# A gated mix of attention and a ReGLU block on one core: padded DRAM rows, down's weights and rows fetched in another order, the last normalisation on GpSimd

## The chip, the cores and the metric

The kernel runs on one core of one Trainium2 chip. The metric is the time of one execution on the device in microseconds; the time before is the median of three runs, 1238.48 us (1235.03 to 1239.87). One more execution was taken with the hardware profiler; all numbers of the trace come from that one.

The core has a matrix engine (TensorE, PE in the profile), VectorE (DVE), ScalarE (ACT) and GpSimd (POOL), each with its own queue of instructions worked off in order, and SyncE (SP), which here only issues DMA transfers, also in order. [...]

## What is computed

```python
# S = 2048 tokens, D = 448, H = 16 heads of 28, F = 1792; all float32
g = sigmoid((x * gate_w).sum(-1, keepdims=True))
q, k, v = heads(A_x @ A_wqkv)
a = concat_heads(softmax(q @ k.T * 28 ** -0.5) @ v) @ A_wo
gate, up = x @ B_W_gate, x @ B_W_up
b = ((gate * (gate > 0)) * up) @ B_W_down
out = g * a + (1 - g) * b
```

## The kernel before

Matrix products of float32 accuracy are made from two parts of each operand. The high part is a rounded copy (`act_high`, line 120, on ScalarE), the low part the rest (`low`, line 126, on VectorE, or `pool_low`, line 129, on GpSimd). Each operand thus passes two engines before TensorE can use it: "split" in what follows.

Three stages follow each other:

1. **Projections** (0 to some 140 us). `qk` (line 420) and `vproj` make q, k and v from X. q and k are split and written to a DRAM tile `qk_d` (line 133), one row of 2048 tokens (8 KB) for each high and each low part of a dimension. The blocks 1 to 3 of X, already split, are written to DRAM tiles `x_d` (line 135) of 128 rows of 8 KB, in 4 chunks of 512 tokens.
2. **Attention with the gate and up products mixed in** (to some 1035 us). There are 32 "visits", two for each head; the string in `ROUNDS` gives the order of small steps of one visit: scores, maxima, exponentials, the product with V, and one pass (`x`) of the gate or up product. At the first score step of an even visit `loads` issues `load_k` (line 164) and `load_q` (line 169) for a later head: K's 56 rows are read twice into partitions 0 to 55 and 56 to 111, Q's rows four times 28. The split gate and up weights `wg` are reloaded from DRAM (`load_f`, line 583) once their buffer is free. At the end of a block of tokens `gu_mm` (line 591) reads the next block of X back, chunk by chunk. The hidden rows h are written to `h_d`.
3. **Down and output** (line 810 on). `down(i)` multiplies hidden row block i (56 of them: 4 blocks of 512 tokens by 14 blocks of 128 features) with down's weights of its feature block: 4 groups of 3 matmuls. `wout(tb, t)` multiplies normalised head outputs with the output weights, 11 matmuls each; `result` mixes both with the gate and writes out.

What orders stage 3 is the list `todo` (line 914), worked off once while the program is built: each engine's queue holds its share of the list in the list's order. Its steps are:

- `fetch_d(i)` (line 868): SyncE loads the raw weight block `wdr` i, if i is below 14, and the hidden row block `hr` i. Each of the two has 4 buffers, so number i waits until number i - 4 has been split.
- `split_wd(i)` (line 700): high part of weight block i on ScalarE, low part on GpSimd. Blocks 0 to 3 were loaded and split before the stage.
- `split_d(i)` (line 876): high part of row block i on ScalarE, low part on VectorE, into one of 3 buffers `hh`, so that it waits for `down(i - 3)`.
- `load_wo` (line 814) and `split_wo` (line 821): output weights, three transfers into `wor`, then split on ScalarE and GpSimd.
- `row_sums(15)` (line 659), `spread(15)` (line 665), `normalise(15)` (line 671): for the last head, the reciprocal of the softmax sums on VectorE, written to DRAM and read back to all partitions (`rb`, four transfers), and the product with them. For the heads before, `normalise` runs on GpSimd; for the last one on VectorE. It ends with four transfers to `o_d`.
- `fetch_o(tb)` (line 829), `split_o(tb, c)` (line 836): the normalised outputs of all heads for 512 tokens, three transfers into `or` (one buffer), split in two halves on ScalarE and GpSimd into `on`.

`before(i, ...)` (line 928) inserts steps ahead of `down(i)`. As the list stands, `normalise(15)` lies ahead of `down(3)`, `fetch_o(0)` ahead of `down(4)`, its splits ahead of `down(6)` and `down(7)`, and the products `wout(0, 0..3)` ahead of `down(9)` to `down(12)`.

Of the kernel before, what the change touches and what calls it, by code (L numbers as in the profile page):

```python
# [8 lines left out]
F32 = mybir.dt.float32  # L9
# [3 lines left out]
OP = mybir.AluOpType  # L13
# [5 lines left out]
P = 128  # L19
S = 2048  # L20
D = 448
H = 16
# [4 lines left out]
NF = F // P  # L27
NB = 4
TB = 512
# [55 lines left out]
def gated_mix_kernel(ctx, tc, x, wq, wo, wgu, wd, out):  # L85
    nc = tc.nc
# [4 lines left out]
    dram = ctx.enter_context(tc.tile_pool(name="dram", bufs=1, space=DRAM))  # L91
# [28 lines left out]
    def act_high(dst, src):  # L120
        nc.scalar.activation(dst, src, AF.Copy)  # L121
# [7 lines left out]
    def pool_low(dst, src, high):  # L129
        nc.gpsimd.tensor_tensor(dst, src, f32(high), op=OP.subtract)  # L130


    qk_d = dram.tile([2 * D, 2, S], F32, name="qk_d")

    x_d = {(tb, r): dram.tile([P, 4, TB], F32, name=f"x_d_{tb}_{r}") for tb in range(1, NB) for r in range(2)}

    v_d = {g: dram.tile([P, NK, 4, 32], F32, name=f"v_d_{g}") for g in (2, 3)}

# [3 lines left out]
    h_d = {}  # L142
# [421 lines left out]
    done = starts[-1] // (2 * NT)  # L564
# [52 lines left out]
    OS, LS = {}, {}  # L617
# [52 lines left out]

    def normalise(h):
        o = OS.pop(h)
        (nc.gpsimd if h < H - 1 else nc.vector).tensor_tensor(o, o, LS.pop(h), op=OP.mult)
        for j in range(NB):
            nc.sync.dma_start(o_d[DH * h:DH * (h + 1), j * TB:(j + 1) * TB], o[32 * j:32 * j + DH])

# [5 lines left out]
    DR, HK, early = {}, {}, []  # L682
# [52 lines left out]
    for v, order in enumerate(ROUNDS):  # L735
# [4 lines left out]
        for o in order:  # L740
# [12 lines left out]
            elif o == "x":  # L753
                i, half, n = passes.pop(0)
# [3 lines left out]
                if n == NT - 1:  # L758
                    i, half, ps = units.pop()
# [15 lines left out]
            elif o == "b":  # L775
                block_min()
            elif o == "A":
                all_max()
            elif o == "g":
                take_max()  # L780
            elif o == "N":
                if v > 1 and v % 2:
                    normalise(v // 2 - 1)
            elif o == "e":
                take_exp()
            elif o in "cf":
                rescale(v, "cf".index(o))
            elif o == "D":
                split_wd(len(early))
                early.append(o)  # L790
            elif o == "l":
                sends.pop()()
            elif o == "u":
                split_f(0, act_high, pool_low, (1,))
                QS.append(last_q("Q2"))
                for a, b in ((GD, 12), (GD + 12, 4)):
                    nc.sync.dma_start(f32(QS[2])[a:a + b].rearrange("p j t -> p (j t)"), Q[1][GD + 2:GD + 2 + b].bitcast(F32))
                load_k(2)
                load_q(2)
                fetch_f(2)  # L800
                parts = 2
            elif o in "PQ":
                pv(v, "PQ".index(o))
# [7 lines left out]
    pf = ctx.enter_context(tc.tile_pool(name="ffn", bufs=1))  # L811
    WO = pf.tile([P, 7, D], F32R, name="WO")

    def load_wo():
        r = pf.tile([P, 4, TB], F32, name="wor", tag="on0", bufs=2)
        nc.sync.dma_start(r[:, 0:3, :D], wo_d[0:3 * P].rearrange("(c p) n -> p c n", p=P))
        for a in (0, 64):
            nc.sync.dma_start(r[a:a + 64, 3, :D], wo_d[3 * P:])
        return r[:, :, :D]

    def split_wo(r):
        act_high(WO[:, 0:3], r[:, 0:3])
        pool_low(WO[:, 3:6], r[:, 0:3], WO[:, 0:3])
        act_high(WO[:, 6], r[:, 3])
        pool_low(WO[64:, 6], r[64:, 3], WO[64:, 6])
# [39 lines left out]

    WD.append(pf.tile([P, NF - 4, 2, D], F32R, name="WD"))

    def fetch_d(i):

        if i < NF:  # L870
            DR[i] = pf.tile([P, D], F32, name=f"wdr_{i}", tag="wdr", bufs=4)
            nc.sync.dma_start(DR[i], wd[i * P:(i + 1) * P])
        HK[i] = pf.tile([P, TB], F32, name=f"hr_{i}", tag="hr", bufs=4)
        nc.sync.dma_start(HK[i], h_d[i])

    def split_d(i):
        HH[i] = pf.tile([P, 2, TB], F32R, name=f"hh_{i}", tag="hh", bufs=3)
# [20 lines left out]
    def down(i):  # L898
# [6 lines left out]
        if f == NF - 1:  # L905
# [5 lines left out]


    wor = []
    todo = [(fetch_d, 4), (fetch_d, 5), (split_d, 0), (row_sums, H - 1), (split_d, 1), (fetch_d, 6), (fetch_d, 7),
            (lambda: wor.append(load_wo()),), (gate_up, done), (split_wd, 4), (spread, H - 1),
            (split_wd, 5), (gate_up, done + 1)]
    for i in range(NB * NF):
        if i >= 4 and i + 4 < NB * NF:
            todo.append((fetch_d, i + 4))
        if i + 2 < NB * NF:  # L920
            if 4 < i + 2 < NF - 1:
                todo.append((split_wd, i + 3))
            todo.append((split_d, i + 2))
        todo.append((down, i))
        if done + 2 + i < NB * NF:
            todo.append((gate_up, done + 2 + i))

    def before(i, *new):
        n = todo.index((down, i))
        todo[n:n] = new  # L930


    before(3, (normalise, H - 1))
    for tb, load, split, at in ((0, 4, (6, 7), (9, 10, 11, 12)), (1, 9, (13, 14), (16, 17, 18, 19)), (2, 21, (23, 25), (28,) * 4),
                                (3, 35, (37, 39), (42,) * 4)):
        before(load, (fetch_o, tb))
        for k, i in enumerate(split):
            before(i, (split_o, tb, 2 * k))
        for t, i in enumerate(at):
            before(i, (wout, tb, t))  # L940
    before(1, (lambda: split_wo(wor[0]),))
    for f, *a in todo:
        f(*a)

# [36 lines left out]
```

## Time and profile before

| | |
|---|---|
| median of three runs | 1238.48 us (1235.03 to 1239.87) |
| the profiled execution: its time | 1232.55 us |
| its span, first to last instruction | 1230.8 us |
| granted TensorE clock, mean | 0.996 |
| TensorE busy | 1198.2 us (97%) |
| VectorE, ScalarE, GpSimd busy | 908.3, 871.0, 750.9 us |
| moved by DMA | 178.36 MB, mean 145 GB/s |

How to read it: a group or timeline row names the line of the kernel, the engine, the operation, then out<-in by the program's tile names. In brackets or behind the last bar stands how long the engine was idle just before, and whose work ended that. `SPq` is SyncE issuing a transfer: its duration is the issue alone, not the transfer. A row "A <- B: 7.8, 1, 7.8" of the waits says that A waited for B 7.8 us in total, once, 7.8 us at the longest. In a table of windows each row gives the busy time of PE, weight loads, VectorE, ScalarE and GpSimd in that stretch, then the granted clock, the share of time that the 16 DMA engines were busy, and the GB/s that they moved.

### The profile page before, as it was taken

The numbers are of one execution on the slowest core, as the hardware profiler recorded it, in microseconds if no ns is written. First come the engines' busy times: TensorE is split into PE (matmuls) and PEld (weight loads), VectorE is DVE, ScalarE is ACT, GpSimd is POOL, SyncE is SP. The second block draws the span as 40 slices with busy tenths as digits, with TensorE's granted clock in tenths as the row PEclk, the third lists the DMA queues.
The fourth block names the chain that finished last, engine by engine and source line by source line (L and its number), as shares of the span: only waits on it lengthen the run. The fifth ranks groups of instructions, "written<-read, shape, count | busy, mean of one in ns | idle before, by whom it ended". The sixth has DMA issues, their size and how long they took to land.

```text
span 1230.8 us, 16835 instructions
## 1 busy us (share of the span) xinstructions
PE 1198.2 (97%) x6183; PEld 825.4 (67%) x6183; DVE 908.3 (74%) x1178; ACT 871.0 (71%) x956; POOL 750.9 (61%) x327
## 2 busy tenths in 40 slices
PE   9999989999999999999999999999999999899998
PEld 6888655565666666656665666566666566789998
DVE  6466788989898888878887988798888553543342
ACT  5322779898999788877887888888887896422121
POOL 4221477989898676666675766767666776441020
PEclk9999999999999999999999999999999999899999
DMA  9846454354445435252545434344423235543432
GB/s 319 301 171 257 148 187 133 123 155 147 160 116 171 131 122 157 71 147 85 147 133 167 122 114 116 116 138 160 137 97 102 96 105 177 185 141 112 138 111 81
DMA packets 63486, 178.36 MB, mean 145 GB/s; under 512 B 13050, under 2 KB 19650, under 8 KB 58754
## 3 DMA queue, kind: packets, MB, share of 16 engines
q1 hardware_dynamic: 56812, 151.53, 40.3%
q0 software_dynamic: 6160, 25.30, 5.4%
q8 instruction: 49, 0.80, 0.3%
q10 hardware_dynamic: 432, 0.46, 0.1%
q14 instruction: 33, 0.27, 0.1%
HBM read 118.58 MB, written 58.87 MB: 144 GB/s over the span
## 4 chain that ended last, share of the span: by engine, by line
PE 81%; DMA 7%; DVE 4%; ACT 3%; issue 1%; SPq 1%; POOL 1%; DVEq 0%; ACTq 0%; POOLq 0%
PE gu L594 18%; PE po L647 18%; PE s L302 16%; PE acc L885 9%; PE sm L200 9%; PE qk L423 5%; DMA wg<-ws_d 4%; PE wo L848 3%; PE v L441 3%; DVE r L256 2%; DVE mx L204 1%; ACT P L308 1%; ACT P L306 1%; DMA X<-x_d 1%; DMA wgr<-wgu 1%
## 5 line engine op out<-in xcount | busy, mean ns | idle before, releaser
L285 POOL TENSOR_TENSOR P<-P,rm 128x2048 f32<-128x2048 f32 x102 | 469.9, 4627 | 110.1 <-DVE rm L279 84.8
L594 PE MATMUL gu<-X,wg 128*128 128x512 f32 x1232 | 365.0, 395 | 6.4 <-DMA wg<-ws_d 6.3
L204 DVE TENSOR_REDUCE mx<-sm 128x1 f32<-128x1024 f32 x256 | 303.1, 1216 | 48.1 <-PE sm L200 46.6
L302 PE MATMUL s<-Q,K 128*128 128x512 f32 x1024 | 319.9, 407 | 7.7 <-ACT P L306 4.0
L594 PEld LDWEIGHTS gu<-X,wg 128*128 128x128 f32 x1232 | 231.7, 188 | 64.3 <-DMA wg<-ws_d 8.5
L302 PEld LDWEIGHTS s<-Q,K 128*128 128x128 f32 x1024 | 181.6, 188 | 99.5 <-ACT P L306 17.0
L308 ACT ACTIVATE P<-s 128x1024 f32<-128x1024 f32 x204 | 200.6, 1031 | 62.4 <-PE s L302 60.6
L647 PE MATMUL po<-P,V 128*32 128x512 f32 x1640 | 227.1, 594 | 0.4 <-ACT rl L604 0.4
L306 ACT ACTIVATE P<-s 128x1024 f32<-128x1024 f32 x206 | 198.8, 1033 | 11.2 <-PE s L302 9.8
L292 ACT ACTIVATE P<-P 128x2048 f32<-128x2048 f32 x102 | 195.8, 1923 | 2.7 <-POOL P L285 2.4
L200 PE MATMUL sm<-K,Q 128*128 128x512 f32 x520 | 167.5, 406 | 7.9 <-DVE rm L279 2.2
L256 DVE SCALAR_TENSOR_TENSOR r<-s,r 128x1024 f32<-128x1024 f32 x124 | 151.8, 1225 | 23.2 <-ACT P L308 10.6
L647 PEld LDWEIGHTS po<-P,V 128*32 128x32 f32 x1640 | 63.1, 110 | 116.6 <-issue 111.9
L647 PE MATMUL po<-V 128*32 128x512 f32 x408 | 135.6, 594 | 0.0
L285 POOL TENSOR_TENSOR V<-V,rm 128x2048 f32<-128x2048 f32 x24 | 111.0, 4633 | 25.3 <-DVE rm L279 19.0
L200 PEld LDWEIGHTS sm<-K,Q 128*128 128x128 f32 x520 | 91.0, 188 | 49.0 <-ACT P L306 14.8
L127 DVE TENSOR_TENSOR hh<-hr,hh 128x512 fp32r<-128x512 f32 x52 | 51.5, 994 | 86.7 <-ACT hh L121 78.2
L121 ACT ACTIVATE hh<-hr 128x512 fp32r<-128x512 f32 x52 | 32.8, 631 | 112.4 <-PE acc L885 112.4
L885 PE MATMUL acc<-WD,hh 128*128 128x448 f32 x480 | 102.9, 374 | 4.3 <-ACT hh L121 3.1
L885 PEld LDWEIGHTS acc<-WD,hh 128*128 128x128 f32 x480 | 92.4, 193 | 13.2 <-ACT hh L121 3.9
L256 DVE SCALAR_TENSOR_TENSOR r<-s,P 128x1024 f32<-128x1024 f32 x50 | 61.1, 1221 | 39.3 <-ACT P L308 38.8
L271 DVE TRANSPOSE_TENSOR_REDUCE mn<-r 128x32 f32<-128x1024 f32 x63 | 78.2, 1241 | 1.4
(88 smaller groups left out, 1139.1 us busy)
## 6 DMA issues: line engine op xcount, KB each, us to landing
wg<-ws_d SPq DMA_DIRECT2D x42, 896.0 KB
K<-qk_d SPq DMA_DIRECT2D x32, 448.0 KB
Q<-qk_d SPq DMA_DIRECT2D x64, 224.0 KB
h_d<-h SPq DMA_DIRECT2D x56, 256.0 KB
hr<-h_d SPq DMA_DIRECT2D x52, 256.0 KB
ws_d<-wg SPq DMA_DIRECT2D x14, 896.0 KB
qk_d<-st POOLq DMA_DIRECT2D x21, 512.0 KB, 3.1
wgr<-wgu SPq DMA_DIRECT2D x13, 512.0 KB
```

The source lines that it names most:

```text
L200: nc.tensor.matmul(ps[:, c, :], Q[h][:, u * P:(u + 1) * P], K[h % 3][:, k0:k0 + TB], start=True, stop=True)
L204: nc.vector.tensor_reduce(to, ps, axis=AX.XY, op=OP.max)
L256: nc.vector.scalar_tensor_tensor(r, ps, -1.0, before, op0=OP.mult, op1=OP.min)
L271: nc.vector.tensor_reduce(MN[:, 1:3], R2.pop((v, j)).rearrange("p a (b r) -> p a b r", r=32), axis=AX.X, op=OP.min, apply_transpose=True)
L285: nc.gpsimd.tensor_tensor(QUAD[q], QUAD[q], m, op=OP.subtract)
L292: nc.scalar.activation(q, q, AF.Exp, scale=-SCALE)
L302: nc.tensor.matmul(ps[:, c], K[h % 3][:, k * P:(k + 1) * P], Q[h][:, j * TB:(j + 1) * TB], start=True, stop=True)
L306: nc.scalar.activation(dst, ps, AF.Exp, scale=SCALE)
L308: nc.scalar.activation(dst, ps, AF.Copy, scale=-1.0)
L594: nc.tensor.matmul(ps, WS[i][:, s, a], xf(i // NF, b), start=(n == 0), stop=(n == NT - 1))
L647: nc.tensor.matmul(po[32 * j:32 * j + 32], V[:, h // 4 % 2, k, h % 4], AT.pop((v, k, j)), start=(k == k0), stop=(k == k0 + NK // 2 - 1))
L885: nc.tensor.matmul(ACC[i // NF][t][:, :D], HH[i][:, a, t * P:(t + 1) * P], wd_high_low(f, b), start=(f == 0 and n == 0), stop=(f == NF - 1 ...
```

## The change

- The rows of `qk_d` and `x_d` in DRAM become 512 bytes (128 floats) longer; the added bytes are neither written nor read.
- `normalise(15)` runs on GpSimd, and stands ahead of `split_wo` and `down(1)` instead of ahead of `down(3)`.
- `fetch_d` is parted into `fetch_w` (raw weights) and `fetch_h` (hidden rows), each placed directly behind the split that frees its buffer. Weight blocks 8 and 9 are fetched right behind `split_wd(4)` and `split_wd(5)`, later ones three `down`s earlier in the list than before; rows 6 and 7 come behind `load_wo` and behind weight block 9, later ones two `down`s earlier in the list.
- `fetch_o(0)` and its two splits, and `fetch_o(1)`, stand one `down` earlier in the list; the places of `wout` among the `down`s are the same.

```diff
-    qk_d = dram.tile([2 * D, 2, S], F32, name="qk_d")
-    x_d = {(tb, r): dram.tile([P, 4, TB], F32, name=f"x_d_{tb}_{r}") for tb in range(1, NB) for r in range(2)}
+    qk_d = dram.tile([2 * D, 2, S + P], F32, name="qk_d")[:, :, :S]
+    x_d = {(tb, r): dram.tile([P, 4 * TB + P], F32, name=f"x_d_{tb}_{r}")[:, :4 * TB].rearrange("p (c t) -> p c t", c=4) for tb in range(1, NB) for r in range(2)}
...
-        (nc.gpsimd if h < H - 1 else nc.vector).tensor_tensor(o, o, LS.pop(h), op=OP.mult)
+        nc.gpsimd.tensor_tensor(o, o, LS.pop(h), op=OP.mult)
...
-    def fetch_d(i):
+    def fetch_w(i):
         if i < NF:
             DR[i] = pf.tile([P, D], F32, name=f"wdr_{i}", tag="wdr", bufs=4)
             nc.sync.dma_start(DR[i], wd[i * P:(i + 1) * P])
-        HK[i] = pf.tile([P, TB], F32, name=f"hr_{i}", tag="hr", bufs=4)
-        nc.sync.dma_start(HK[i], h_d[i])
+
+    def fetch_h(i):
+        if i < NB * NF:
+            HK[i] = pf.tile([P, TB], F32, name=f"hr_{i}", tag="hr", bufs=4)
+            nc.sync.dma_start(HK[i], h_d[i])
...
-    todo = [(fetch_d, 4), (fetch_d, 5), (split_d, 0), (row_sums, H - 1), (split_d, 1), (fetch_d, 6), (fetch_d, 7),
-            (lambda: wor.append(load_wo()),), (gate_up, done), (split_wd, 4), (spread, H - 1),
-            (split_wd, 5), (gate_up, done + 1)]
+    todo = [(fetch_w, 4), (fetch_h, 4), (fetch_w, 5), (fetch_h, 5), (split_d, 0), (row_sums, H - 1), (split_d, 1),
+            (fetch_w, 6), (fetch_w, 7), (lambda: wor.append(load_wo()),), (fetch_h, 6), (gate_up, done), (spread, H - 1),
+            (split_wd, 4), (fetch_w, 8), (split_wd, 5), (fetch_w, 9), (fetch_h, 7), (gate_up, done + 1)]
     for i in range(NB * NF):
-        if i >= 4 and i + 4 < NB * NF:
-            todo.append((fetch_d, i + 4))
+        if 5 < i + 3 < NF:
+            todo += [(split_wd, i + 3), (fetch_w, i + 7)]
         if i + 2 < NB * NF:
-            if 4 < i + 2 < NF - 1:
-                todo.append((split_wd, i + 3))
             todo.append((split_d, i + 2))
+        if i >= 2:
+            todo.append((fetch_h, i + 6))
         todo.append((down, i))
...
-    before(3, (normalise, H - 1))
-    for tb, load, split, at in ((0, 4, (6, 7), (9, 10, 11, 12)), (1, 9, (13, 14), (16, 17, 18, 19)), (2, 21, (23, 25), (28,) * 4),
+    for tb, load, split, at in ((0, 3, (5, 6), (9, 10, 11, 12)), (1, 8, (13, 14), (16, 17, 18, 19)), (2, 21, (23, 25), (28,) * 4),
                                 (3, 35, (37, 39), (42,) * 4)):
...
-    before(1, (lambda: split_wo(wor[0]),))
+    before(1, (normalise, H - 1), (lambda: split_wo(wor[0]),))
```

## The prediction

> **What bounds the kernel now.** I read the page's busy times and clock line first, then the matmul timeline of the last stage, then who was late there (ScalarE, then SyncE's queue), and last the stage with q and k.
>
> ```profile
> span 1230.8 us, 16835 instructions
> ...
> PE 1198.2 (97%) x6183; PEld 825.4 (67%) x6183; DVE 908.3 (74%) x1178; ACT 871.0 (71%) x956; POOL 750.9 (61%) x327
> ...
> PEclk9999999999999999999999999999999999899999
> ```
>
> TensorE is busy for 1198.2 of 1230.8 us, so only some 32 us of idle time can be won, plus what a lowered clock costs (the 8 near the end of the clock line). The change touches two places where TensorE stands. The first is the start of the down stage. In the timeline the columns are start, duration, then the instruction, and in brackets the idle time before it:
>
> ```profile
> 1055.20 7.46 PE L885 MATMUL acc<-WD,hh 128*128 128x448 f32 x36
> 1063.88 0.68 PE L885 MATMUL acc<-WD,hh 128*128 128x448 f32 x2 [1.22 <-ACT hh L121]
> 1065.12 3.84 PE L885 MATMUL acc<-WD,hh 128*128 128x448 f32 x10 [0.57 <-DVE hh L127]
> 1070.86 0.68 PE L885 MATMUL acc<-WD,hh 128*128 128x448 f32 x2 [1.89 <-ACT hh L121]
> 1072.11 3.77 PE L885 MATMUL acc<-WD,hh 128*128 128x448 f32 x10 [0.58 <-DVE hh L127]
> 1075.72 2.02 PE L848 MATMUL wo<-WO,on 128*128 128x448 f32 x9
> 1078.70 0.68 PE L848 MATMUL wo<-WO,on 128*128 128x448 f32 x2 [0.95 <-POOL on L130]
> 1079.21 0.97 PE L885 MATMUL acc<-WD,hh 128*128 128x448 f32 x4
> ...
> 1066.00:1070.00 4.00, 2.97 (x9) 2.31 (x7) 0.00 (x0) 0.28 (x1) 0.00 (x0) 0.68 0.97 293
> ```
>
> Each `down` is 12 matmuls. The 36 of `down` 4 to 6 take 7.46 us, 2.43 us for 12 with the overlap off. `down(7)`, `down(8)` and the first output product then fill 1062.66 to 1079.21: 16.55 us for 2.43 + 2.43 + 2.23 (11 matmuls) = 7.1 us of work. So 9.45 us are lost, 5.21 of them idle. The rest is mostly the clock: the last row (a window; behind the five engines stand clock, DMA share and GB/s) has a granted clock of 0.68, and ten matmuls take 3.84 instead of about 2.1 us, 1.7 too many. ScalarE tells what is late:
>
> ```profile
> 1062.73 0.58 ACT L121 ACTIVATE WD<-wdr 128x448 fp32r<-128x448 f32 x1 [6.70 <-DMA wdr<-wd]
> 1063.21 0.61 ACT L121 ACTIVATE hh<-hr 128x512 fp32r<-128x512 f32 x1
> 1069.71 0.58 ACT L121 ACTIVATE WD<-wdr 128x448 fp32r<-128x448 f32 x1 [5.89 <-DMA wdr<-wd]
> 1070.72 1.04 ACT L121 ACTIVATE on<-or 128x1024 fp32r<-128x1024 f32 x1
> ```
>
> ScalarE waits twice for a raw block of down's weights (blocks 8 and 9), and the split of the row that TensorE needs is queued behind. SyncE says why they are late:
>
> ```profile
> 1042.03 0.43 SPq L816 DMA_DIRECT2D wor<-wo_d  x1
> 1044.72 2.74 SPq L669 DMA_DIRECT2D rb<-l_d  x4
> 1049.88 0.34 SPq L613 DMA_DIRECT2D h_d<-h  x1
> 1058.05 1.98 SPq L675 DMA_DIRECT2D o_d<-os  x4
> 1060.13 0.36 SPq L872 DMA_DIRECT2D wdr<-wd  x1
> 1061.01 0.42 SPq L832 DMA_DIRECT2D or<-o_d  x1
> 1062.71 0.54 SPq L872 DMA_DIRECT2D wdr<-wd  x1
> 1068.01 0.32 SPq L874 DMA_DIRECT2D hr<-h_d  x1
> ...
> SPq L675 <- DVE os L673: 7.8, 1, 7.8
> SPq L874 <- DMA or<-o_d: 2.5, 2, 2.2
> SPq L613 <- DMA wor<-wo_d: 2.4, 1, 2.4
> ```
>
> SyncE stands 7.8 us for the last normalisation, with the load of block 8 queued behind it (issued 1060.13, used 1062.73: 2.6 us), and block 9 follows the 1 MB of `or` (three transfers, 768 KB and twice 128 KB by their tiles; block 9 issued 1062.71, used 1069.71: 7.0 us). The last row shows a second limit: `h_d` at 1049.88 is the eighth transfer after the first of `wor` (1042.03) and waited until that had landed, so this queue has eight in flight at most.
>
> **The change, part by part.** *Weights further ahead.* `fetch_w(8)` and `(9)` now stand in the queue directly behind `spread`, before the normalised rows. Their buffers are those of blocks 4 and 5, split long before. They are eighth after the second and third part of `wor`. Without two row loads (512 KB) ahead of it `wor` lands somewhat earlier than 1049.8, so blocks 8 and 9 issue at about 1049 and land 2.6 us later, by 1052; both waits on `wdr` (6.70 and 5.89 us of ScalarE) go. The row loads wait for a `hh` split of the same round, but the row is used four rounds (9.7 us) later, so that wait is covered by four `down`s.
>
> *The normalisation on GpSimd.*
>
> ```profile
> 1056.38 1.65 DVE L673 TENSOR_TENSOR os<-os,rb 128x512 f32<-128x512 f32 x1
> ...
> 1029.46 1.29 POOL L673 TENSOR_TENSOR os<-os,rb 128x512 f32<-128x512 f32 x1
> ...
> 1051.24 4.67 POOL L130 TENSOR_TENSOR WO<-wor,WO 128x1344 fp32r<-128x1344 f32 x2 [7.26 <-ACT WO L121]
> 1055.99 3.05 POOL L130 TENSOR_TENSOR WD<-wdr,WD 128x448 fp32r<-128x448 f32 x2
> ...
> 1071.84 2.47 POOL L130 TENSOR_TENSOR on<-or,on 128x1024 fp32r<-128x1024 f32 x1 [0.32 <-ACT on L121]
> ```
>
> It costs 1.29 us there and waits only for `rb`. No row shows that landing: it lies between the end of the issue plus 2.6 us (1050.1) and 1056.38, when VectorE used it. I take 1050.4, since VectorE was busy with other rows until then. Behind it on GpSimd wait the low halves of `WO` (4.67) and of weight blocks 6 and 7 (3.05 for two): 1050.4 + 1.29 + 4.67 + 1.5 = 1057.9 for block 6. TensorE needs it at `down(6)`, 1060.2, so 2.3 us of cover hide the move. The four writes to `o_d` issue at 1051.7 to 1053.7 instead of 1058.05.
>
> *The head outputs' load.* `fetch_o(0)` stands behind `fetch_w(10)`, which needs block 6's buffer (1057.9), and `fetch_h(9)`: `or` issues at about 1058.8, 2.2 us earlier than now. Its landing: 7.0 us (1061.01 to 1068.01, where SyncE waited for it) is the upper end; the lower is 4.2 us, an estimate of 2.1 (the 2.6 of block 8 without the 0.5 that its 224 KB take at the 440 GB/s quoted below) and 768 KB at 440 GB/s. I take 5.7: the four `o_d` writes are no longer just ahead of it. So it lands at 1064.5.
>
> *What is late next.* `split_o(0, 0)` moved one `down` forward, so on ScalarE weight block 9 and row 8 are now queued behind its wait for `or`. ScalarE: `on` until 1065.5, `WD`, then `hh` done at 1066.6, its low half on VectorE 1.2 later (the idle brackets above: about 0.6 between pairs), 1067.8. TensorE ends `down(7)` at 1065.1, stands 1.5 us, does two matmuls, stands again, and ends `down(8)` at 1067.8 + 2.05 = 1069.85. Twice such a stop was followed by the low clock (1.7 us); I charge half, 0.85: 1070.7. GpSimd meanwhile: first half of `on` 1065.5 + 2.47, block 9 1.4, second half 2.6: 1072.0; the tenth matmul of the product comes at 1070.7 + 1.8 = 1072.5, covered. The product ends at 1070.7 + 2.23 = 1072.95 instead of 1079.21: **6.2 us won**. With `or` after 4.2 us, everything is 1.5 earlier, without the low clock and with a 0.4 wait for GpSimd: 8.1. With 7.0 us and the full clock cost: 4.1.
>
> *The longer rows.* The second place:
>
> ```profile
> 413.40 0.87 SPq L167 DMA_DIRECT2D K<-qk_d  x2
> 415.03 3.16 SPq L175 DMA_DIRECT2D Q<-qk_d  x4
> 418.29 0.48 SPq L586 DMA_DIRECT2D wg<-ws_d  x1
> ...
> 418.50:423.00 4.50, 4.50 (x20) 3.20 (x18) 4.29 (x9) 4.50 (x7) 1.64 (x1) 1.00 0.99 226
> 434.50:436.50 2.00, 2.00 (x26) 0.55 (x20) 1.66 (x2) 2.00 (x3) 0.00 (x0) 1.00 1.05 440
> 1035.00:1036.00 1.00, 1.00 (x6) 0.81 (x5) 0.30 (x1) 0.74 (x2) 0.67 (x1) 1.00 0.87 165
> ...
> PE gu L594 <- DMA wg<-ws_d: 6.3, 5, 2.1
> PE sm L200 <- DMA X<-x_d: 1.3, 2, 0.6
> ```
>
> While a head's K and Q come in (1.79 MB, about 9 us), the 16 DMA engines are fully busy and move 226 GB/s; `wg` is queued behind, and five times TensorE waits for it. The bounds of the padding are nothing and 6.3 + 1.3 = 7.6 us. The nearest row for a row pitch that is a power of two is the second window: the reload of V, 8 KB rows at a pitch of 8 KB, runs at 440 GB/s. It differs from K and Q in filling 128 partitions where they fill 56 or 28, not in its pitch. So I take 0.
>
> [...]
>
> **The sum.** Against the profiled execution's 1232.55 us: minus 6.2 gives 1226.35. That execution lies 5.93 below the median shown (1238.48, of 1235.03 to 1239.87), so I put the median at 1232.3.
>
> **The rivals.** *The padding works too.* For it: the third window above, the start of a `wg` load into 128 partitions with 7 KB rows, moves only 165 GB/s, so not the partitions alone make a load slow, and engines that start together might meet in DRAM. Against it: the V row. It would take away the 7.6: 1224.7.
>
> *The stall only moves.* GpSimd's chain holds `fetch_w(10)`, and with it `or`, and ScalarE is stuck on `or` with row 8 behind it. If `rb` lands 2 us late and `or` takes 7.0, the gain is 2.1: 1236.4. Against it: nothing in the queue at that time but two small loads.
>
> *Slower: the gaps between rows cost bandwidth.* K's 56 rows are one run of DRAM now and are apart afterwards. Should K and Q fall to the 165 GB/s of the third window, their 9 us become 12.3, and each of the five waits grows by 3.3: 16.5 us lost, 1248.8. It decides from about 2.5 us a wait (12.4 in all, the 6.2 won and 6.2 more). Against it: every row is still 8 KB in one piece.
>
> **How the numbers follow.** About 0.5% (6.2 us) is what a measurement can tell from no change, and the forecast lies on that line. Chances: forecast 55% (its own range 1230.4 to 1234.4), padding too 28%, stall moves 9%, slower 8%. Faster: half the forecast and nearly all of the second, 0.54; same: the other half and the third, 0.36; slower 0.10 with what I overlook. The range 1223.5 to 1240 leaves out the slower case and the best end of the second.
>
> **What would show it.** Right: no wait of ScalarE on `wdr`, blocks 8 and 9 issued before `o_d`, the normalisation on GpSimd near 1051, `or` issued near 1059, one stop of TensorE of about 2 us before `down(8)` with row 8 behind `on`, and the first output product done near 1073. The five `wg` waits unchanged at about 6 us and some 226 GB/s in the K and Q windows mean that the padding does nothing; under 2 us of such waits mean that the first rival holds. The forecast is wrong if TensorE stands elsewhere in the down stage, or if those waits grow.

## The result and the profile after

| | before | after |
|---|---|---|
| median (lowest to highest), 12 runs each | 1236.65 us (1230.54 to 1239.87) | 1236.12 us (1232.35 to 1239.58) |
| ratio of after to before, 95% interval | | 1.0002 (0.9983 to 1.0021) |
| the profiled execution: time, span | 1232.55, 1230.8 us | 1237.06, 1235.2 us |

The change moves nothing that can be measured. The time lies inside the predicted range, 3.8 us above the forecast, and close to what the rival "the stall only moves" gave (1236.4); how much of that is luck is said with the prediction's steps further down. The profiled execution of before was a quick one among its own runs, that of after was not, so in what follows times of the last stage are counted from the first matmul of `down(0)`, which is 1045.47 us in before and 1047.74 us in after.

The page of after, its busy times and clock line:

```profile
span 1235.2 us, 16834 instructions
...
PE 1200.2 (97%) x6183; PEld 825.6 (67%) x6183; DVE 910.1 (74%) x1177; ACT 870.6 (70%) x956; POOL 752.9 (61%) x328
...
PEclk9999999999999999999999999999999999899999
```

The dip near the end of the clock line is still there. TensorE's timeline in the down stage shows why (start, duration, instruction, and in brackets the idle time before it):

```profile
1072.61 1.11 PE L889 MATMUL acc<-WD,hh 128*128 128x448 f32 x2 [5.25 <-ACT hh L121]
1074.61 4.10 PE L889 MATMUL acc<-WD,hh 128*128 128x448 f32 x10 [0.89 <-DVE hh L127]
1078.51 2.51 PE L848 MATMUL wo<-WO,on 128*128 128x448 f32 x11
```

Before, TensorE stood at five places of this stretch, 5.21 us together; now it stands at two, 6.14 us together, both at `down(8)`: ahead of its first matmul and behind its second. The first output product ended 33.9 us after the start of `down(0)` (1079.38); now it ends at 1081.02, after 33.3 us. ScalarE's timeline, then its waits in the stretch from 1047 to 1085 us (total, times, longest), say what is late:

```profile
1060.10 0.63 ACT L121 ACTIVATE hh<-hr 128x512 fp32r<-128x512 f32 x1 [1.33 <-PE acc L889]
1070.51 1.06 ACT L121 ACTIVATE on<-or 128x1024 fp32r<-128x1024 f32 x1 [9.78 <-DMA or<-o_d]
1071.47 0.56 ACT L121 ACTIVATE WD<-wdr 128x448 fp32r<-128x448 f32 x1
1071.94 0.61 ACT L121 ACTIVATE hh<-hr 128x512 fp32r<-128x512 f32 x1
```
```profile
ACT on L121 <- DMA or<-o_d: 9.8, 1, 9.8
```

The two waits for raw weights, 6.70 and 5.89 us, are gone, as intended. In their place is one of 9.78 us for `or`, and the split of row 8, which TensorE needs for `down(8)`, stands third behind it. SyncE's timeline and its waits show how `or` came to be late:

```profile
1043.63 0.43 SPq L816 DMA_DIRECT2D wor<-wo_d  x1
1044.11 1.15 SPq L818 DMA_DIRECT2D wor<-wo_d  x2
1045.31 0.58 SPq L878 DMA_DIRECT2D hr<-h_d  x1
1045.99 1.04 SPq L613 DMA_DIRECT2D h_d<-h  x1
1047.13 4.17 SPq L669 DMA_DIRECT2D rb<-l_d  x4
1051.40 0.84 SPq L872 DMA_DIRECT2D wdr<-wd  x2
...
1055.62 1.61 SPq L675 DMA_DIRECT2D o_d<-os  x4
1057.32 0.34 SPq L878 DMA_DIRECT2D hr<-h_d  x1
1061.79 0.36 SPq L872 DMA_DIRECT2D wdr<-wd  x1
1062.24 0.38 SPq L878 DMA_DIRECT2D hr<-h_d  x1
1062.67 0.42 SPq L832 DMA_DIRECT2D or<-o_d  x1
```
```profile
SPq L872 <- POOL WD L130: 12.4, 2, 8.4
...
SPq L669 <- DMA wor<-wo_d: 2.3, 1, 2.3
```

Count the transfers from the first of `wor` (1043.63): three of `wor`, row 6, the store of h, and three parts of `rb` are eight. The fourth part of `rb` is the ninth, and waited 2.3 us for the first of `wor` to land (1050.98). In before row 6 did not stand there, the four parts were the fifth to the eighth, and the transfer that waited (2.4 us) was the ninth, a store of h. The wait in after did not make `rb` late, though. The trace also records when each transfer landed. The first three parts, which had not waited, landed 5.5 to 6.0 us after the start of `down(0)`, the fourth 6.3 us after it (1054.05). In before the four landed after 5.8 to 6.4 us (the last at 1051.85), so no earlier. GpSimd, which needs all four, starts its product 0.25 us behind the last of them, and then does one thing after another:

```profile
1054.30 1.29 POOL L673 TENSOR_TENSOR os<-os,rb 128x512 f32<-128x512 f32 x1 [8.04 <-DVE hh L127]
1055.55 4.66 POOL L130 TENSOR_TENSOR WO<-wor,WO 128x1344 fp32r<-128x1344 f32 x2
1060.29 4.14 POOL L130 TENSOR_TENSOR WD<-wdr,WD 128x448 fp32r<-128x448 f32 x3
```

The bracket of the first row names a split on VectorE, which ended at 1054.16, 0.1 us behind the landing of `rb`. ScalarE had the high part of `WO` ready at 1052.79, so GpSimd stood 1.5 us with that work at hand, because the product was ahead of it in its queue.

Weight block 10 (issued 1061.79) takes the buffer of block 6, whose low half is the first of those three `WD`. So SyncE stood from 1057.66 (the end of the row load at 1057.32) to 1061.79 (the shorter of the two waits for `POOL WD`, 12.4 - 8.4 = 4.0 us), with `or` queued behind, though the stores to `o_d` had been issued by 1057.23. The windows, with five engines, clock, DMA share and GB/s:

```profile
1058.00:1062.00 4.00, 4.00 (x22) 3.70 (x21) 3.99 (x3) 1.40 (x3) 3.84 (x4) 1.00 0.26 71
1062.70:1070.50 7.80, 4.66 (x23) 3.97 (x22) 0.00 (x0) 0.00 (x0) 1.73 (x2) 1.00 0.88 253
1071.00:1078.50 7.50, 5.00 (x12) 3.97 (x13) 5.91 (x3) 4.94 (x9) 6.86 (x4) 0.56 0.37 125
1080.00:1110.00 30.00, 30.00 (x146) 27.24 (x146) 13.19 (x16) 6.33 (x10) 10.63 (x9) 1.00 0.46 145
418.50:423.00 4.50, 4.50 (x20) 3.19 (x18) 4.29 (x9) 4.50 (x7) 1.64 (x1) 1.00 0.97 217
```

First row: while SyncE waited, the DMA engines were idle three quarters of the time. Second: then they were 0.88 busy, with block 10 and row 9 (224 and 256 KB, by their tiles) just ahead of `or`. Third: after the stop the clock was 0.56. The fourth is used in the last section. The last row is that of the K and Q load, about as before (226 GB/s); V's reload still moves 433 GB/s. So are the waits for gate and up weights (7.2 us in all, against 6.3):

```profile
PE gu L594 <- DMA wg<-ws_d: 7.2, 5, 2.1
```

### The profile page after: what moved, and what is told of

Its sections match the earlier page's. It is cut to its first block, busy times and chain, and to the rows that moved or that the text cites. A ratio compares the mean times of both kernels' runs of the same rounds, so it can differ in the third digit from the quotient of the medians.

```text
span 1235.2 us, 16834 instructions
## 1 busy us (share of the span) xinstructions
PE 1200.2 (97%) x6183; PEld 825.6 (67%) x6183; DVE 910.1 (74%) x1177; ACT 870.6 (70%) x956; POOL 752.9 (61%) x328
## 4 chain that ended last, share of the span: by engine, by line
PE 81%; DMA 6%; DVE 6%; ACT 4%; issue 1%; POOL 1%; SPq 1%; DVEq 0%; ACTq 0%; POOLq 0%
PE gu L594 18%; PE po L647 18%; PE s L302 16%; PE sm L200 9%; PE acc L889 8%; PE qk L423 5%; DMA wg<-ws_d 4%; PE wo L848 3%; PE v L441 3%; DVE r L256 2%; DVE mx L204 1%; ACT P L308 1%; ACT P L306 1%; DMA wor<-wo_d 1%; DMA or<-o_d 1%
## 5 line engine op out<-in xcount | busy, mean ns | idle before, releaser
L256 DVE SCALAR_TENSOR_TENSOR r<-s,r 128x1024 f32<-128x1024 f32 x124 | 151.8, 1225 | 23.2 <-ACT P L308 10.6
L200 PEld LDWEIGHTS sm<-K,Q 128*128 128x128 f32 x520 | 91.1, 189 | 49.6 <-ACT P L306 15.5
L127 DVE TENSOR_TENSOR hh<-hr,hh 128x512 fp32r<-128x512 f32 x52 | 54.4, 1056 | 86.9 <-ACT hh L121 86.9
```

The source lines that it names most:

```text
L200: nc.tensor.matmul(ps[:, c, :], Q[h][:, u * P:(u + 1) * P], K[h % 3][:, k0:k0 + TB], start=True, stop=True)
L256: nc.vector.scalar_tensor_tensor(r, ps, -1.0, before, op0=OP.mult, op1=OP.min)
```

## The experiments

Twelve kernels ran. The table puts them side by side. "Ratio" is against runs of the kernel before on the same chip (1235.3 to 1237.1 us median). The columns behind it come from one profiled execution each. "`or` issued" counts from the start of `down(0)`. The stretch from there to the start of the last `down` matmul holds 847 spacings; at 202.7 ns, the usual one, they are 171.7 us, and what the stretch took beyond that divides into TensorE's idle time, the loss in stretches of half clock, and wider spacings at full clock (for before 171.7 + 5.2 + 3.4 + 1.0 = 181.3 us). The last two columns are good to some 0.3 us. The start of `down(0)` itself lies between 1045.2 and 1051.0 us in these executions, so the stretch is compared, and not the total of a profiled execution.

| kernel | median us | ratio (95%) | `or` issued | idle | half clock | wider |
|---|---|---|---|---|---|---|
| before | | | 15.5 | 5.2 | 3.4 | 1.0 |
| after | 1236.12 | 1.0002 (0.9983 to 1.0021) | 14.9 | 6.4 | 2.8 | 2.5 |
| pad_only | 1236.24 | 0.9991 (0.9975 to 1.0007) | 16.0 | 6.2 | 3.4 | 1.0 |
| k_spread | 1235.84 (one run) | | 15.6 | 4.9 | 3.5 | 0.9 |
| fetch_only | 1236.62 | 1.0005 (0.9985 to 1.0025) | 15.0 | 4.5 | 3.5 | 3.1 |
| norm_only | 1230.88 | 0.9949 (0.9929 to 0.9970) | 11.2 | 2.7 | 3.1 | 3.7 |
| split_67 | 1235.97 | 1.0001 (0.9987 to 1.0016) | 14.7 | 5.2 | 1.7 | 3.6 |
| split_later | 1231.88 | 0.9960 (0.9944 to 0.9975) | 14.7 | 2.2 | 0 | 1.1 |
| dve_norm | 1231.17 | 0.9966 (0.9949 to 0.9984) | 11.7 | 3.2 | 1.7 | 0.7 |
| or_ahead | 1227.08 | 0.9921 (0.9899 to 0.9944) | 9.7 | 0.1 | 0 | 2.0 |
| ahead_nopad | 1226.07 | 0.9926 (0.9906 to 0.9946) | 10.4 | 1.8 | 0 | 0.8 |
| ahead_dve | 1227.18 | 0.9938 (0.9920 to 0.9956) | 10.2 | 0.1 | 0 | 0.6 |
| ahead_old | 1229.31 | 0.9960 (0.9944 to 0.9976) | 10.2 | 2.8 | 1.7 | 4.0 |
| fetch_ahead | 1227.22 | 0.9939 (0.9910 to 0.9967) | 10.6 | 1.2 | 0 | 3.2 |

### The longer rows alone (pad_only)

The two edits of `qk_d` and `x_d`, on the kernel before.

> The kernel before with the longer rows of q, k and X and nothing else. Theory (row pitch is not what slows K and Q): no change, within 0.2%, five waits of TensorE for wg of 6 to 7.5 us in sum, and about 220 GB/s while K and Q come in. Rival (the padding works, and the rest of the change took its gain away): 5 to 8 us faster, wg waits under 2 us, well over 300 GB/s in those windows.

1236.24 us, ratio 0.9991: no change. Its windows of the K and Q load and its waits for gate and up weights:

```profile
414.50:418.50 4.00, 4.00 (x19) 3.23 (x18) 3.73 (x4) 3.59 (x5) 4.00 (x2) 1.00 0.72 182
418.50:423.00 4.50, 4.50 (x20) 3.43 (x19) 4.29 (x7) 4.50 (x6) 2.65 (x1) 1.00 0.96 213
```
```profile
PE gu L594 <- DMA wg<-ws_d: 6.8, 5, 1.8
```

K's load was issued 1.0 us later in this execution than in before (414.39 against 413.40), which by itself lowers the first row. Moved by 1 us, the two windows show 209 and 223 GB/s, against 219 and 226 in before. K and Q move no faster, and the five waits stay: 6.8 us, where the kernels with rows of the old length show 5.6 (norm_only) to 9.0 us (fetch_only). The longer rows do nothing that can be measured, and they do no harm either: the rival of costly gaps falls too.

### K into every second partition (k_spread)

```diff
-            nc.sync.dma_start(f32(K[h % 3])[a:a + 2 * DH], k)
+            nc.sync.dma_start(f32(K[h % 3])[a // (2 * DH):4 * DH:2], k)
```

K's rows then lie in other partitions than the rows of Q that they are multiplied with, so the scores are not those of the task; the bytes that are moved, and their places in DRAM, are the same.

> The kernel before with K's 56 rows loaded into every second partition (0, 2, ... 110, then 1, 3, ... 111) instead of 0 to 55 and 56 to 111: what is computed with K is not the reference's, the bytes and their places in DRAM are the same. Theory (the partitions that are written bound these loads): while K comes in (about 414.5 to 417) the rate rises from some 220 to over 300 GB/s, and the waits for wg fall by 1 us or more in sum. Rival (it is the reading side, or the many short transfers): 200 to 240 GB/s as before, wg waits of 6 to 8 us.

```profile
414.50:418.50 4.00, 4.00 (x19) 3.16 (x17) 3.79 (x4) 3.76 (x3) 4.00 (x2) 1.00 0.82 219
```

This window, in which K comes in, shows 219 GB/s, in before as well. K's two transfers landed 4.9 and 6.3 us after their issue, in before 4.6 and 6.3. The waits for gate and up weights, 8.5 us, are no shorter either. That the partitions that are written bound these loads, the theory of this run, is not borne out: with K in every second partition the rate did not rise. Why this load stays at half of the rate of V's reload (441 GB/s in this run) is open.

### The parts of the change by themselves (norm_only, fetch_only)

norm_only is before with the normalisation on GpSimd and ahead of `down(1)`; the fetches stay in the old order:

```diff
-        (nc.gpsimd if h < H - 1 else nc.vector).tensor_tensor(o, o, LS.pop(h), op=OP.mult)
+        nc.gpsimd.tensor_tensor(o, o, LS.pop(h), op=OP.mult)
...
-    before(3, (normalise, H - 1))
...
-    before(1, (lambda: split_wo(wor[0]),))
+    before(1, (normalise, H - 1), (lambda: split_wo(wor[0]),))
```

> The kernel before with one part of the change: the last normalisation on GpSimd and ahead of down(1); fetches, splits and rows as before. Theory (SyncE's 8 us wait for the normalisation was the root of the stops, and the new fetch order and the earlier split give the gain away again): the normalised rows are written some 5 us earlier, blocks 8 and 9 follow, TensorE stands under 2.5 us in the down stage instead of 5.2, and the kernel is 4 to 8 us faster than before, also faster than the whole change. Rival (without the new fetch order block 9 still comes behind the head outputs' load and is late): the two stops stay above 4 us in sum, within 0.3% of before.

1230.88 us: this part alone gains. SyncE's and TensorE's timelines:

```profile
1053.80 1.60 SPq L675 DMA_DIRECT2D o_d<-os  x4
1055.50 0.36 SPq L872 DMA_DIRECT2D wdr<-wd  x1
...
1056.38 0.42 SPq L832 DMA_DIRECT2D or<-o_d  x1
```
```profile
1067.43 0.70 PE L885 MATMUL acc<-WD,hh 128*128 128x448 f32 x2 [2.06 <-ACT hh L121]
1068.69 4.10 PE L885 MATMUL acc<-WD,hh 128*128 128x448 f32 x10 [0.56 <-DVE hh L127]
```

`or` goes out 11.2 us after the start of `down(0)` instead of 15.5, behind weight block 8, which waits for nothing there. One stop of the two is gone; the other, for block 9 behind `or`, is left. The profile shows 2.5 us less idle time. Over its ten runs the mean granted clock was 0.9943, over the 25 of before beside it 0.9920, and 0.0023 of 1235 us is 2.8 us. Together that is a little more than the 4.6 us between the medians (1235.50 to 1230.88), but it adds one trace to means of many runs, so where the gain lies is indicated and not shown: between the two profiled executions the stretch is the same (181.1 and 181.3 us), because norm_only's has 2.7 us more of the wider spacing. GpSimd's timeline bears on `rb`:

```profile
1052.47 1.30 POOL L673 TENSOR_TENSOR os<-os,rb 128x512 f32<-128x512 f32 x1 [8.78 <-DMA h_d<-h]
```

Here row 6 does not stand ahead of `rb`, and all four parts were issued by 1.5 us after the start of `down(0)`. Still the last of them landed only after 7.1 us (1052.31; the bracket names the store of h, which was landing just then), and the product starts after 7.3, later than in after (6.6).

fetch_only is before with the change's order of fetches, its normalisation and its splits as they were.

> The kernel before with one part of the change: the new order of the fetches of down's weights and rows; normalisation on VectorE ahead of down(3), head outputs loaded and split where they were. Theory: ScalarE's two waits for raw weights go, but the head outputs' load comes no earlier than before (about 16 us after down(0) begins), so TensorE now stands at the first output product, 4 to 7 us in sum; within 0.4% of before. Rival (weights were the cause, and the rest of the change spoils it): TensorE stands under 2 us, 5 us or more faster.

1236.62 us, ratio 1.0005: nothing. `or` is issued 15.0 us after the start. ScalarE has no wait for weights in the down stage any more, and TensorE stands for the head outputs instead, three times in the first output product, at the longest 3.0 us for GpSimd's low half of `on`.

So of the change's two parts for this stage one gains 4.6 us and one nothing, and together they gain nothing. The new order takes the gain away: in after, `or` stands behind weight block 10, which must wait for GpSimd, and GpSimd is busy with the normalisation and `WO`. The next runs move each link of that chain.

### The splits of `on` later (split_later, split_67)

After, with the first two `split_o` ahead of `down(9)` and `down(10)` and the products at 12, 12, 13, 13 (split_later), or the splits at 6 and 7 and the products where they were (split_67):

```diff
-    for tb, load, split, at in ((0, 3, (5, 6), (9, 10, 11, 12)), (1, 8, (13, 14), (16, 17, 18, 19)), (2, 21, (23, 25), (28,) * 4),
+    for tb, load, split, at in ((0, 3, (9, 10), (12, 12, 13, 13)), (1, 8, (13, 14), (16, 17, 18, 19)), (2, 21, (23, 25), (28,) * 4),
```

> The changed kernel with the splits of the first head outputs ahead of down(9) and down(10) instead of down(5) and down(6), and their products ahead of down(12) and down(13). Theory (ScalarE stands in order on the load of the head outputs, and row 8 is queued behind it): the stop of 5.2 + 0.9 us before down(8) goes, with it the two half-clock stretches (3.4 us) and the slower matmul spacing after them (about 2 us): 8 to 11 us faster than the changed kernel, about 1226 us; ScalarE still waits for that load or no longer, but nobody waits for ScalarE. Rival (down's rows or weights are late too, behind GpSimd's chain and SyncE's queue): TensorE stops elsewhere before down(12), and less than 4 us are won.

> The changed kernel with the first head outputs split ahead of down(6) and down(7) as before the change. Theory (the load of the head outputs is too late for its products, wherever ScalarE waits for it): no stop before down(8), but one of 4 to 7 us in sum at the first output product; 0 to 3 us faster than the changed kernel. Rival (only row 8's place behind the split hurts): TensorE stands under 2.5 us, 6 us or more faster than the changed kernel.

split_later gains 0.40% on before: with `or` as late as in after (14.7 us), row 8 is not behind it any more. Its median lies 4.2 us below that of after, half of the 8 to 11 us expected, and just above the bound of 4 that the rival had. In the profiled executions the stretch shrinks by 8.4 us (183.4 to 175.0), about what was expected; why the median shows half of it is open. Its timeline of TensorE has only short stops, none followed by the half clock (its windows from 1045 to 1222 us all show 1.00):

```profile
1075.84 0.68 PE L889 MATMUL acc<-WD,hh 128*128 128x448 f32 x2 [0.41 <-ACT hh L121]
1076.79 4.81 PE L889 MATMUL acc<-WD,hh 128*128 128x448 f32 x22 [0.28 <-DVE hh L127]
1081.44 2.02 PE L848 MATMUL wo<-WO,on 128*128 128x448 f32 x9
1084.94 0.47 PE L848 MATMUL wo<-WO,on 128*128 128x448 f32 x1 [1.48 <-POOL on L130]
```

split_67 gains nothing (1235.97). Row 8 is ahead of `on` there, but the product ahead of `down(9)` then finds `on` unfinished. TensorE's timeline:

```profile
1070.15 1.08 PE L848 MATMUL wo<-WO,on 128*128 128x448 f32 x4 [0.80 <-ACT on L121]
1072.08 1.29 PE L848 MATMUL wo<-WO,on 128*128 128x448 f32 x5 [0.86 <-ACT on L121]
1076.90 1.05 PE L848 MATMUL wo<-WO,on 128*128 128x448 f32 x2 [3.53 <-POOL on L130]
```

The stops have about the same size (5.2 us together) in another place. With `or` late, splits and products must both move.

### The normalisation on VectorE, in the new order (dve_norm)

After, with line 673 as in before.

> The changed kernel with the last normalisation on VectorE as before, everything else as changed. Theory (the place of the normalisation matters little, since the head outputs' load waits for the later of two things): normalisation ends about 1 to 3 us later than on GpSimd, weight block 6 is split about 1.3 us earlier, the load issues within 1.5 us of the changed kernel's, the stop before down(8) stays at 4.5 to 7.5 us, the time within 0.3%. Rival (GpSimd's longer chain makes the stop): the load issues 2 us or more earlier, and 4 us or more are won.

It came out faster than after, 1231.17 us, which I had not expected. SyncE's timeline, and the normalisation in VectorE's:

```profile
1056.07 1.61 SPq L675 DMA_DIRECT2D o_d<-os  x4
...
1058.64 0.36 SPq L872 DMA_DIRECT2D wdr<-wd  x1
...
1059.57 0.42 SPq L832 DMA_DIRECT2D or<-o_d  x1
```
```profile
1053.62 2.42 DVE L673 TENSOR_TENSOR os<-os,rb 128x512 f32<-128x512 f32 x1 [1.79 <-DMA rb<-l_d]
```

The product is slower on VectorE here (2.42 us, in after 1.29 on GpSimd) and the stores go out 0.4 us later than in after, each counted from `down(0)`. But GpSimd neither waits for `rb` nor does the product ahead of `WO` (it starts `WO` 4.6 us after `down(0)`, in after 7.8), so it gets to block 6 sooner: block 10 is issued 10.8 us after `down(0)` (1058.64 - 1047.83) where after has 14.1, and `or` 3.2 us earlier. That the normalisation stood on GpSimd, ahead of the work that frees the buffer, is what held `or` in the new order.

### The fetch of the head outputs directly behind the stores (or_ahead and four relatives)

After, with `or` taken out from behind block 10:

```diff
-        before(load, (fetch_o, tb))
+        if tb:
+            before(load, (fetch_o, tb))
...
-    before(1, (normalise, H - 1), (lambda: split_wo(wor[0]),))
+    before(1, (normalise, H - 1), (fetch_o, 0), (lambda: split_wo(wor[0]),))
```

> The changed kernel with the load of the first head outputs put in SyncE's queue directly behind the normalised rows, ahead of weight block 10. Theory (the load is late because it waits in SyncE's queue for the buffer of weight block 6, which GpSimd splits last): it issues some 4 us earlier, about 1 to 2 us after the writes of the normalised rows, lands 3 to 5 us earlier, and the stop before down(8) shrinks from 6.1 us to under 2.5: 4 to 8 us faster than the changed kernel, 1228 to 1232 us. Rival (the load itself is slow, 7 to 8 us whatever its place, or it waits for the writes to land): under 2 us won.

1227.08 us, ratio 0.9921: 0.8% faster than before, 9 us faster than after, a little more than the 4 to 8 expected. TensorE's and ScalarE's timelines:

```profile
1046.87 9.89 PE L889 MATMUL acc<-K,hh 128*128 128x448 f32 x48
1056.60 12.44 PE L889 MATMUL acc<-WD,hh 128*128 128x448 f32 x60
1068.88 2.40 PE L848 MATMUL wo<-WO,on 128*128 128x448 f32 x11
```
```profile
1062.23 1.07 ACT L121 ACTIVATE on<-or 128x1024 fp32r<-128x1024 f32 x1 [2.36 <-DMA or<-o_d]
```

TensorE does not stop, ScalarE waits 2.36 us instead of 9.78, and no stretch of half clock is left in the stage. The first product ends 24.4 us after the start of `down(0)` (1071.28), 8.9 us earlier than in after.

Four more kernels take parts away from this one: the longer rows (ahead_nopad); GpSimd (ahead_dve, normalisation on VectorE); the new order of weights and rows (ahead_old: norm_only with `or` directly behind the stores, so with the splits of `on` at their old places too); and rows and GpSimd together (fetch_ahead).

> The kernel after with the first attention rows fetched directly behind the normalisation's stores (as in the run with the fetch ahead, 1227.1 us, ratio 0.992), but with the rows of q, k and X of the old length. Theory (the longer rows do nothing, also where the tail no longer hides anything): 1227 us, within 1.5, ratio 0.990 to 0.995, TensorE idle in the down stage under 1 us. Rival (the longer rows help, and only the tail's stop had hidden it): 1230 or more, with the waits for gate and up weights longer by 2 us or more.

> The kernel after with the first attention rows fetched directly behind the normalisation's stores, and the normalisation on VectorE instead of GpSimd, at the same place of the order. Theory (what counts is that the fetch is issued before the weight block that waits for GpSimd, not which engine normalises): on VectorE the stores went out 8.24 us after down(0) began against 7.88 on GpSimd, so the fetch about 0.4 us later than the 9.74 us of the run with the fetch ahead; ScalarE waits about 2.8 us for it instead of 2.36, TensorE does not stop: 1227 us, within 1.5. [...]

> The kernel before with the normalisation on GpSimd ahead of the second down product and the first attention rows fetched directly behind its stores, but the old order of the fetches of weights and rows, old splits and old row lengths. Theory (the weights fetched further ahead are what lets the attention rows go first): weight block 8 and row 8 are now issued behind the three transfers of the attention rows, 1.6 us later than in the run with the normalisation alone, where block 9's landing already held ScalarE for 7.2 us and TensorE for 2.6; so ScalarE waits for a weight block by 5 us or more, TensorE stops 2.5 to 6 us, 1230 to 1235 us. Rival (the order of the weights' fetches plays no part, all of the gain is the early attention rows): TensorE idle in the down stage under 1 us, 1227 us within 1.5.

> Of the change only the new order of the fetches, with the normalisation moved ahead of the second down product but on VectorE, the rows at their old length, and the first attention rows fetched directly behind the normalisation's stores. Theory (the place of that fetch and the weights fetched further ahead make the whole gain; neither the longer rows nor GpSimd is needed): 1226.5 us, within 1.5, ratio 0.991 to 0.9945, in the down stage TensorE idle under 2 us and no stretch at the half clock. Rival (each of the two parts left out adds a little to the gain): 1229 or more, ratio 0.995 or above.

Without the longer rows 1226.07, with VectorE 1227.18, without both 1227.22 us: within their intervals the same time. Neither part plays a role that these intervals, 0.2 to 0.3% to either side, can show once `or` goes first. Idle time in ahead_nopad was 1.8 us, more than the 1 us that I had allowed; no half clock followed (the ten matmuls behind its longest stop, 1.35 us, took 2.30 us). ahead_old comes in at 1229.31 us, a little below the 1230 expected, with the stop that was expected. The waits of its ScalarE from 1047 to 1085 us:

```profile
ACT WD L121 <- DMA wdr<-wd: 8.5, 2, 6.9
```

In the old order the raw weights are late again, now behind `or`. Its ratio (0.9960) and those of the four others (0.9921 to 0.9939) have intervals that touch or overlap, so what the new order adds to the early `or`, some 2 to 3 us, is indicated by the trace more than measured by the time. The interval of norm_only (0.9949), which has neither the new order nor the early `or`, overlaps with theirs too.

The least change among these runs that has the gain is thus fetch_ahead: fetch weights further ahead, normalise ahead of `down(1)` on either engine, and issue `or` at once.

## Why the prediction went as it did

- **The longer rows: right.** The term was 0; pad_only measured 0.9991, and ahead_nopad that the tail had hidden nothing. The first rival, with 28%, fell, and so did the one with a loss. One reading behind the term was off: V's rows differ from those of Q in their pitch too (8 KB against 16 KB), and only from those of K they do not. The runs carry the point without it.
- **Weights further ahead: right.** Blocks 8 and 9 are issued 3.7 us after `down(0)` (1051.40; forecast about 3.5), and both waits on `wdr` are gone.
- **The normalisation on GpSimd: right in its price (1.29 us), wrong in its start.** The prediction had only bounds for the landing of `rb` and took a time near the early one, 4.9 us after `down(0)`. The product started after 6.6 us. The landings in the trace of before put `rb` at 6.4 us there already, those of after at 6.3, so the time taken was 1.5 us short for either kernel. The 2.3 us that its last part waited for the first of `wor`, since row 6 has its new place, do not explain it: norm_only has no such wait, and its `rb` landed after 7.1 us. The chain behind it ran as worked out, 1.6 us late: `or` issued after 14.9 instead of 13.3 us.
- **The load of `or`: too short.** 5.7 us were taken, because the stores are not just ahead of it any more. But block 10 and row 9 are, 480 KB, issued 0.4 to 0.9 us ahead, as block 8 and row 8 were in before. It took 7.8 us (1062.67 to 1070.49), above the upper end of 7.0. In or_ahead, with the stores just ahead of it and neither block nor row, it took 5.6 us (1056.61 to 1062.23). By the landings, it took 6.6 to 7.8 us in the eight other kernels that have a block and a row just ahead of it, before among them, and 4.7 to 5.9 directly behind the stores in ahead_dve, ahead_old and fetch_ahead; in the last two four and more loads followed within 4 us, so it is not the loads behind. ahead_nopad does not fit: 7.6 us behind the stores, unexplained.
- **What is late next: the right place, the wrong size.** The single stop ahead of `down(8)`, with row 8 behind `on` on ScalarE, is exactly there. Forecast were 1.5 us and a second, shorter one; the stop is 5.25 and 0.89 us, because 1.6 and 2.1 us of lateness went straight into it. The clock was charged at 0.85 us, and took 2.8.
- **The term of the sum that failed** is therefore the 6.2 us won at the first output product. It measured 0.6 us (33.9 to 33.3 us after `down(0)`). It failed at two times that went into it, the landing of `rb` and the length of the load of `or`, and at the price of the clock.
- **The rival "the stall only moves"**, with 9%, named this mechanism and both conditions, `rb` 2 us late (1.4 measured) and `or` 7.0 us long (7.8). The evidence against it ("two small loads") spoke against neither: `rb` landed no earlier in before, and with a block and a row just ahead of it `or` took 6.6 to 7.8 us. It deserved more than 9%.
- **The time itself is in part luck.** The range of 1223.5 to 1240 had room for no change as well as for the forecast gain, and "faster", with 0.54, did not come. The rival's 1236.4 is close because the prediction put the median 5.93 us above the profiled execution, from three runs. Over the twelve runs it lies 4.10 above (1236.65 - 1232.55); with that the forecast would be 1230.5 and the rival's time 1234.6.

Open: why after's time equals before's although its profiled stage took 2.1 us more (183.4 to 181.3). Most of that is wider spacing (2.5 to 1.0 us), and with one trace of each kernel it cannot be told whether this belongs to the kernel or to the execution.

## What to carry to other kernels

Before moving a load earlier in an in-order queue, list what stands between it and its data: here a prefetch that waited for GpSimd held the one urgent load for 4 us while the DMA engines were busy for a quarter of the time (0.26), and putting the urgent load first was worth 0.8%, where the prefetch by itself was worth nothing. Where a step hangs on when a load lands, read the landing from the trace before taking a time near one end of its bounds: here that was 1.5 us short, and everything behind it inherited the error. Two edits of which one alone gains and which together do nothing should be run apart.

## What the runs showed of the hardware

- **The half clock came in steps of 3.41 us, and in the down stage with short stops.** In the clock records of before and after, the stretches at 0.5 but the one that the end of the program cuts last 3.41 us (from 966.14, 1065.13 and 1071.96 in before, from 658.86 and 969.47 in after) or twice that (6.83 us from 1071.87 in after), and in each of the two traces their starts lie a whole number of 3.41 us apart. In the down stage they cost 1.7 us each in before, and 2.8 us for the 6.83 in after. The half clock followed stops of 1.8 us in all (1.22 and 0.57 in before), and of 1.5 (0.95 and 0.58 in ahead_old, where the next 22 matmuls took 6.29 us), but not the single stops of 1.48 (split_later) or 1.35 us (ahead_nopad). In split_67 the stops of 0.80 and 0.86 us, 1.7 in all, were not followed either (the five matmuls behind them took 1.29 us). What makes the difference is not shown.
- **Matmuls back to back had two spacings at full clock,** some 202.7 and 206.7 ns (means over 10 us in before and after). The window from 1080 to 1110 us counts 149 matmuls in before and 146 in after; the wider one persisted for 120 us and more (norm_only, 147 in each 30 us from 1080 to 1200), and came in or_ahead too (147 from 1110 to 1140), where TensorE stood only 0.1 us in the stage. By the last column of the table wider spacings cost 0.6 to 4.0 us in this stage; their cause is open.
- **A late issue hardly moved a landing.** The parts of `rb` in after were issued from 1047.13 to 1051.00, 3.9 us apart, and landed within 0.8 us (1053.27 to 1054.05), behind the `wor` transfers issued before them. The 2.3 us that the last part waited in the queue hardly moved its landing: 0.27 us behind the third part, where before has 0.21 without the wait.
